# Six operations in place of seven for VectorE's share of a softmax exponential

## The chip, the cores and the metric

The kernel runs on one core of a Trainium2 chip. The metric is the device time of one execution in microseconds (us); a figure for a kernel is the median of its runs. The engines of the core are written as the profile writes them: PE (TensorE, matrix products), ACT (ScalarE, activation functions), DVE (VectorE, elementwise work), POOL (GpSimd) and SP (SyncE, which issues transfers here).

## What is computed

Two blocks are run on the same input x of 2048 tokens by 512 features, in bf16, and mixed by a gate per token:

```python
g = sigmoid((x * gate_w).sum(-1, keepdims=True))
# a: attention, 32 heads of 16 features
qkv = (x @ wqkv) split into q, k, v
p = softmax((q @ k^T) * 16 ** -0.5)        # 32 heads x 2048 x 2048
a = (p @ v) @ wo
# b: feed-forward, 1792 wide
b = (silu(x @ w_gate) * (x @ w_up)) @ w_down
out = g * a + (1 - g) * b
```

The expensive part is the exponential in the softmax: 32 x 2048 x 2048 = 134 million of them. A head has only 16 features, so the matrix products around an exponential are small beside it.

## The kernel before

**Units and blocks.** The attention is cut into 32 units: a unit is one of 4 blocks of 512 queries together with one of 8 groups of 4 heads. In a unit there are 16 key tiles of 128 keys and 4 heads, so 64 score blocks of 128 keys x 512 queries; over all units 2048 score blocks. A score block is one matrix product with a 64-row weight (`score`, L607), its exponential, and one matrix product with the values that adds into the unit's output `o_ps` in PSUM (`pv`, L719). The softmax denominators come from a column of ones in the values.

**Two ways to an exponential.** Most blocks go in pairs to ACT (`emit_pair`, L620): two scores are written into one of two PSUM buffers `s_t` (128x1024), and one ACTIVATE with Exp makes the bf16 tile `e_t` of both. The rest goes to DVE (`emit_d`, L640): the score block is written into the single PSUM buffer `d_t`, and `first` (L659) turns it into an integer in `y_t`, which holds four such blocks (128x2048, uint16, three buffers). The integer is a bf16 bit pattern with two additional fraction bits: score x 512 log2(e) / 4, plus 512 x 127. Read as it is, its nine low bits are the fraction of the power of two, and a straight line between powers of two stands in for 2^fraction. Seven operations on the whole 128x2048 tile then correct that line by a cubic in the fraction and drop the two additional bits: the fraction `z_t` is masked out (L670), three operations and one more product make the correction `u_t` (L671 to L676), it is added to `y_t` (L677), and a multiplication by 0.25 leaves the bf16 pattern (L678), which `pv` reads as bf16. `z_t` and `u_t` have one buffer each.

**Who decides on the order.** The kernel's Python writes the order of PE, ACT and DVE by hand: `ordered` (L145) chains each instruction to the one before it on its engine. A planner keeps a clock for each engine (`plan.pe`, `plan.act`, `plan.dve`) and adds a cost written in the source for every instruction emitted. The numbers at the head of each entry of `vops` (0.73 for an operation on one tensor, 1.26 for one on two, L670 to L678) are such costs. `fill_dve` (L694) gives DVE its next piece of work whenever its clock is behind PE's: first a waiting `d_t`, then an owed piece of the side work, then one of the `vops`. `to_vector` (L1085) decides whether the next score block goes to DVE: never in the first unit, only in a unit's first 50 blocks (the first 4 in the last unit), only while fewer than three `y_t` are in work and the costs left in `vops` sum to at most 6:

```python
if not un or at_ > (50 if un < UNITS - 1 else 4) or y_live[0] >= 3 or sum(v[0] for v in vops) > 6:
    return 0
return 1
```

So the costs in `vops` set, when the kernel is built, how many of the 2048 blocks go to DVE. A finished `y_t` is put on the list `late`, and its four value products are emitted once the planner's clock says that it is ready: into the open unit's `o_ps`, or, where the unit has closed, into a buffer `x_ps` of its own, which DVE adds to the unit's sum (L747).

**Side work.** The projections of q, k and v, the gate, the feed-forward block (`gu_chain`, `down_pieces`), the normalization and the output projection are cut into pieces with due times, and `Pacer` (L47) feeds them to PE in between. They take a Tanh on ACT (`th`, L557) and evacuations from PSUM on DVE (`gs`, `mt`, `bblk` and others). PE runs its instructions in order, so a product that waits for DVE holds up the scores behind it.

Of the kernel before, what the change touches and what calls it, by code (L numbers as in the profile page):

```python
# [9 lines left out]
ALU = mybir.AluOpType  # L10
# [68 lines left out]
def kernel(  # L79
# [37 lines left out]

    EXP_A = 512.0 * inv_sqrt_dh * math.log2(math.e)  # L120
    EXP_B = 512.0 * 127.0

    EXP_C3, EXP_C2, EXP_C1, EXP_S = 0.0012034477878222, 1.8215637461803453, -1248.848130748923, 1.0 / 4096.0

# [41 lines left out]
    vec = Ordered()  # L168
# [53 lines left out]
    for i in range(2):  # L222
        nc.vector.tensor_copy(
            out=wpad[i][:, :, :].rearrange("p dc (j c) -> p dc j c", c=32)[:, :, :, 1:1 + DH],
# [14 lines left out]
    for h in range(8):  # L239
# [6 lines left out]
                            op0=ALU.is_gt, op1=ALU.mult)  # L246
    nc.vector.scalar_tensor_tensor(out=bsel[:, :], in0=lo_t[:], scalar=0.5, in1=far_t[:],
                                   op0=ALU.is_lt, op1=ALU.mult)
# [34 lines left out]
    def spend(mode, mms, ready=0.0):  # L283

        plan.pe = max(plan.pe + (0.1 if mode != plan.mode else 0.0), ready) + (0.226 if mode == "F" else 0.216) * mms
        plan.mode = mode
# [320 lines left out]
    def score(ps, b):  # L607
        n, j = b // 4, HEADS[b % 4]
        (qb, g), kt = UNIT[n // KT], n % KT
        r = slice(64 * (j // 2), 64 * (j // 2) + 64)  # L610
        q = q0[qb][r, j % 2, :] if g == 0 else get_qx(qb, g // 2)[r, j % 2, g % 2, :]
        mm(ps, lhsT=kaug[r, g, kt * P:(kt + 1) * P], rhs=q, start=True, stop=True,
           tile_position=(64 * (j // 2), 0))
# [26 lines left out]
    def emit_d(b):  # L640
        while d_wait:
            pay_d()
        d_t = ps_d.tile([P, QBW], F32, tag="d", name="d_t")
        score(d_t[:, :], b)
        spend("R", 1, d_end[0])
        if not vcur:
            y_live[0] += 1
            blocks[b // (4 * KT)] = blocks.get(b // (4 * KT), 0) + 1
            vcur["y"] = vex.tile([P, NV * QBW], U16, tag="y", name="y_t", bufs=3)
            vcur["i"], vcur["b"] = 0, []  # L650
        y, i = vcur["y"], vcur["i"]
        vcur["i"] += 1
        vcur["b"].append(b)
        e_of[b] = y[:, i * QBW:(i + 1) * QBW].bitcast(BF16)
        block = dict(vcur)
        if i == NV - 1:
            vcur.clear()

        def first():  # L659
            vec.tensor_scalar(out=y[:, i * QBW:(i + 1) * QBW], in0=d_t[:, :], scalar1=EXP_A, scalar2=EXP_B,  # L660
                              op0=ALU.mult, op1=ALU.add)
            if i < NV - 1:
                return
            z = vex.tile([P, NV * QBW], U16, tag="z", name="z_t")
            u = vex.tile([P, NV * QBW], F16, tag="u", name="u_t")
            ya, za, ua = y[:, :], z[:, :], u[:, :]
            mine = list(block["b"])
            assert sorted(m % 4 for m in mine) == list(range(4)) and mine[0] // (4 * KT) == mine[-1] // (4 * KT)
            vops.extend([
                (0.73, lambda: vec.tensor_scalar(out=za, in0=ya, scalar1=0x1FF, scalar2=None, op0=ALU.bitwise_and)),  # L670
                (0.73, lambda: vec.tensor_scalar(out=ua, in0=za, scalar1=EXP_C3, scalar2=EXP_C2, op0=ALU.mult,  # L671
                                                 op1=ALU.add)),
                (1.26, lambda: vec.tensor_tensor(out=ua, in0=ua, in1=za, op=ALU.mult)),
                (0.73, lambda: vec.tensor_scalar(out=ua, in0=ua, scalar1=EXP_C1, scalar2=EXP_S, op0=ALU.add,
                                                 op1=ALU.mult)),
                (1.26, lambda: vec.tensor_tensor(out=ua, in0=ua, in1=za, op=ALU.mult)),  # L676
                (1.26, lambda: vec.tensor_tensor(out=ya, in0=ya, in1=ua, op=ALU.add)),  # L677
                (0.73, lambda: (vec.tensor_scalar(out=ya, in0=ya, scalar1=0.25, scalar2=None, op0=ALU.mult),  # L678
                                late.append((plan.dve + 0.4, mine)))),
            ])  # L680
        d_wait.append((plan.pe + 0.25, first))

    def pay_d():
        ready, f = d_wait.pop()
        plan.dve = max(plan.dve, ready) + 0.6
        f()
        d_end[0] = plan.dve + 0.1
# [189 lines left out]
    for i in range(2):  # L877
# [6 lines left out]
        if i == 0:  # L884
            vec.tensor_scalar(out=kneg1, in0=bsel0, scalar1=kpart0[:, 0:1], scalar2=None, op0=ALU.mult)
            vec.tensor_scalar(out=aq0[:, :].bitcast(U16), in0=q0r[:, :].bitcast(U16), scalar1=0x7FFF, scalar2=None,
                              op0=ALU.bitwise_and)
    vec.scalar_tensor_tensor(out=kneg0, in0=bsel0, scalar=kpart0[:, 1:2], in1=kneg1,
                             op0=ALU.mult, op1=ALU.min)
# [5 lines left out]
    for v in range(2):  # L895
        vec.scalar_tensor_tensor(out=q0[0][:, v, :], in0=bp0[:, :], scalar=vsel[:, v:v + 1],
                                 in1=q0[0][:, v, :], op0=ALU.mult, op1=ALU.add)
# [321 lines left out]
```

## Time and profile before

The kernel before takes 885.43 us (median of three runs, 884.97 to 886.7). The profiled execution has a span of 883.3 us.

| Engine | busy, us | share of the span | instructions |
|---|---|---|---|
| ACT | 853.5 | 97% | 955 |
| DVE | 797.8 | 90% | 1129 |
| PE | 784.8 | 89% | 5078 |
| POOL | 7.0 | 1% | 29 |

The first 20 us hold the loads and the first projections; then ACT starts on exponentials. After the last exponential, which starts at 873.5 us, come the last normalization, the output projection and the stores. A row of the costliest groups reads: line, engine, operation, the tile written and the tile read with shapes and types, the count; then the summed busy time and the mean of one; then the engine's idle time just before these instructions and what ended it. Instructions on one engine overlap a little, so that the mean of one can be larger than the distance from start to start. L157, L160 and L166 are the lines of the three helpers that emit every PE, ACT and DVE instruction; the tiles tell them apart.

### The profile page before, as it was taken

How to read it: one execution, taken by the hardware profiler on the slowest of the kernel's cores; microseconds unless marked ns; L12 is line 12 of the kernel's file. 1: busy time of each engine (PE TensorE's matmuls, PEld its weight loads, DVE VectorE, ACT ScalarE, POOL GpSimd, SP SyncE). 2: the span in 40 equal slices, each digit the busy share in tenths (PEclk: the TensorE clock that was granted, in tenths of full speed). 3: DMA queues.
4: the chain of work that ended last, by engine and by line, in shares of the span. 5: the costliest groups of instructions: out<-in, count | busy, mean ns of one | idle time of the engine just before them, and what ended most of it. 6: DMA issues, size and time to landing. Idle time of an engine off the chain costs nothing.

```text
span 883.3 us, 14242 instructions
## 1 busy us (share of the span) xinstructions
PE 784.8 (89%) x5078; PEld 207.2 (23%) x5168; DVE 797.8 (90%) x1129; ACT 853.5 (97%) x955; POOL 7.0 (1%) x29
## 2 busy tenths in 40 slices
PE   6999999999998898889998888998988888989876
PEld 2222222222222222222222222222222222222211
DVE  6379999999999999998999999999999999999995
ACT  3999999999999999999999999999999999999995
POOL 3000000000000000000000000000000000000000
PEclk9999999999999999999999999999999999999998
DMA  8401021121101112110001112100011111000000
GB/s 208 108 1 33 23 50 43 34 49 28 34 7 31 34 43 64 45 34 16 5 11 35 38 42 61 48 24 10 4 32 34 36 51 44 22 11 5 4 21 24
DMA packets 87535, 31.98 MB, mean 36 GB/s; under 512 B 75120, under 2 KB 87016, under 8 KB 87464
## 3 DMA queue, kind: packets, MB, share of 16 engines
q1 hardware_dynamic: 86408, 30.94, 14.3%
q8 instruction: 40, 0.66, 0.3%
q10 hardware_dynamic: 1056, 0.13, 0.1%
q14 instruction: 31, 0.25, 0.1%
HBM read 20.83 MB, written 2.34 MB: 26 GB/s over the span
## 4 chain that ended last, share of the span: by engine, by line
ACT 40%; PE 29%; DVE 17%; issue 10%; SPq 1%; DMA 1%; DVEq 0%; ACTq 0%
ACT e_t L160 37%; PE s_t L157 11%; DVE y_t L166 7%; PE o_ps L157 6%; DVE u_t L166 5%; ACT th L160 3%; PE d_t L157 3%; PE dps L157 2%; PE gp L157 2%; PE qp L157 1%; PE up L157 1%; SPq L173 1%; DVE mt L166 1%; PE kp L157 1%; DVE gs L166 1%
## 5 line engine op out<-in xcount | busy, mean ns | idle before, releaser
L160 ACT ACTIVATE e_t<-s_t 128x1024 bf16<-128x1024 f32 x890 | 830.3, 1080 | 7.0 <-PE s_t L157 6.0
L157 PE MATMUL s_t<-qx,kaug 64*128 64x512 bf16 x1668 | 333.3, 385 | 59.9 <-ACT e_t L160 55.8
L166 DVE TENSOR_SCALAR y_t<-d_t 128x512 uint16<-128x512 f32 x268 | 184.0, 687 | 28.0 <-PE d_t L157 25.1
L157 PEld LDWEIGHTS <-kaug 64*128 64x128 bf16 x2048 | 99.3, 93 | 389.3 <-issue 387.6
L157 PE MATMUL o_ps<-e_t,vaug 128*32 128x512 bf16 x1780 | 173.1, 388 | 0.9
L166 DVE TENSOR_TENSOR u_t<-u_t,z_t 128x2048 f16<-128x2048 f16 x134 | 163.4, 1219 | 1.9
L157 PE MATMUL d_t<-qx,kaug 64*128 64x512 bf16 x252 | 95.0, 377 | 1.7 <-DVE y_t L166 1.3
L166 DVE TENSOR_TENSOR y_t<-y_t,u_t 128x2048 uint16<-128x2048 uint16 x67 | 81.6, 1218 | 0.8
L157 PEld LDWEIGHTS <-vaug 128*32 128x32 bf16 x2048 | 45.4, 94 | 136.8 <-issue 133.2
L157 PE MATMUL dps<-wd_t,mt 128*128 128x512 bf16 x200 | 62.4, 384 | 3.3 <-issue 3.3
L157 PE MATMUL gp<-xT,wg 128*128 128x512 bf16 x196 | 61.6, 384 | 2.5 <-issue 2.5
L157 PE MATMUL up<-xT,wu 128*128 128x512 bf16 x210 | 62.4, 383 | 1.5 <-issue 1.4
L166 DVE TENSOR_SCALAR y_t<-y_t 128x2048 uint16<-128x2048 uint16 x67 | 46.2, 690 | 1.3
L166 DVE TENSOR_SCALAR u_t<-z_t 128x2048 f16<-128x2048 uint16 x67 | 46.0, 686 | 0.6
L166 DVE TENSOR_SCALAR u_t<-u_t 128x2048 f16<-128x2048 f16 x67 | 45.8, 684 | 0.2
L166 DVE TENSOR_SCALAR z_t<-y_t 128x2048 uint16<-128x2048 uint16 x67 | 45.9, 685 | 0.1
L166 DVE SCALAR_TENSOR_TENSOR gs<-th,gp 128x512 bf16<-128x512 bf16 x56 | 38.2, 682 | 5.1 <-ACT th L160 4.4
L166 DVE SCALAR_TENSOR_TENSOR mt<-gs,up 128x512 bf16<-128x512 bf16 x56 | 38.2, 683 | 3.5 <-PE up L157 1.7
L160 ACT ACTIVATE th<-gp 128x512 bf16<-128x512 f32 x56 | 36.8, 657 | 0.0
L157 PEld LDWEIGHTS <-mt 128*128 128x128 bf16 x263 | 16.2, 99 | 43.8 <-issue 36.8
L157 PE MATMUL s_t<-on,kaug 64*128 64x512 bf16 x112 | 22.0, 384 | 3.3 <-ACT e_t L160 3.2
L166 DVE TENSOR_TENSOR osb<-of,x_ps 128x512 bf16<-128x512 f32 x28 | 19.1, 681 | 2.8 <-PE x_ps L157 2.7
(101 smaller groups left out, 337.8 us busy)
## 6 DMA issues: line engine op xcount, KB each, us to landing
wg<-in_B_w_gate_dram SPq DMA_DIRECT2D x56, 128.0 KB
wu<-in_B_w_up_dram SPq DMA_DIRECT2D x56, 128.0 KB
on<-osb SPq DMA_DIRECT2D x120, 16.0 KB
rb<-rr SPq DMA_DIRECT2D x15, 128.0 KB
wd_t<-in_B_w_down_dram SPq DMA_DIRECT2D x1, 1792.0 KB
qx<-qst SPq DMA_DIRECT2D x112, 16.0 KB
out_dram<-o_t SPq DMA_DIRECT2D x12, 128.0 KB
kaug<-on SPq DMA_DIRECT2D x20, 64.0 KB
```

The costliest lines, as they stand in the source:

```text
L157: ordered(nc.tensor.matmul(*args, **kw))
L160: ordered(nc.scalar.activation(*args, **kw))
L166: return lambda *a, **kw: ordered(f(*a, **kw))
L173: nc.sync.dma_start_transpose(out=xT[:, dc, :], in_=x[:, dc * P:(dc + 1) * P])
```

## The change

The cubic correction is written in another form. Instead of a polynomial in the fraction z by Horner's steps, it uses w = z + 2048, made from the masked integer by an OR with 0x800 in the same instruction, and takes w times the square of a linear term of w. The square needs no further constant in between, so the operation that added C1 and scaled drops out. The constant that the new form leaves over is taken out in the last operation, where an addition joins the multiplication by 0.25, and in `EXP_B`. Seven operations on a 128x2048 tile become six; four of the six stand on the same tiles with the same shapes as before. The planner's cost list gets shorter by its 0.73. The line numbers below line 117 shift by one.

```diff
-    EXP_B = 512.0 * 127.0
-    EXP_C3, EXP_C2, EXP_C1, EXP_S = 0.0012034477878222, 1.8215637461803453, -1248.848130748923, 1.0 / 4096.0
+    EXP_K, EXP_M, EXP_D = 0.0005430666826427128, -1.2590564982977572, -43.5
+    EXP_B = 512.0 * 127.0 + (-44.13360029727899 - EXP_D)
...
-                (0.73, lambda: vec.tensor_scalar(out=za, in0=ya, scalar1=0x1FF, scalar2=None, op0=ALU.bitwise_and)),
-                (0.73, lambda: vec.tensor_scalar(out=ua, in0=za, scalar1=EXP_C3, scalar2=EXP_C2, op0=ALU.mult,
+                (0.73, lambda: vec.tensor_scalar(out=za, in0=ya, scalar1=0x1FF, scalar2=0x800, op0=ALU.bitwise_and,
+                                                 op1=ALU.bitwise_or)),
+                (0.73, lambda: vec.tensor_scalar(out=ua, in0=za, scalar1=EXP_K, scalar2=EXP_M, op0=ALU.mult,
                                                  op1=ALU.add)),
-                (1.26, lambda: vec.tensor_tensor(out=ua, in0=ua, in1=za, op=ALU.mult)),
-                (0.73, lambda: vec.tensor_scalar(out=ua, in0=ua, scalar1=EXP_C1, scalar2=EXP_S, op0=ALU.add,
-                                                 op1=ALU.mult)),
+                (1.26, lambda: vec.tensor_tensor(out=ua, in0=ua, in1=ua, op=ALU.mult)),
                 (1.26, lambda: vec.tensor_tensor(out=ua, in0=ua, in1=za, op=ALU.mult)),
                 (1.26, lambda: vec.tensor_tensor(out=ya, in0=ya, in1=ua, op=ALU.add)),
-                (0.73, lambda: (vec.tensor_scalar(out=ya, in0=ya, scalar1=0.25, scalar2=None, op0=ALU.mult),
+                (0.73, lambda: (vec.tensor_scalar(out=ya, in0=ya, scalar1=EXP_D, scalar2=0.25, op0=ALU.add,
+                                                  op1=ALU.mult),
                                 late.append((plan.dve + 0.4, mine)))),
```

## The prediction

> **What bounds the kernel now.** I first read the busy shares of the engines and their course over the span, on the profile's page.
>
> ```profile
> PE 784.8 (89%) x5078; PEld 207.2 (23%) x5168; DVE 797.8 (90%) x1129; ACT 853.5 (97%) x955; POOL 7.0 (1%) x29
> ...
> DVE  6379999999999999998999999999999999999995
> ACT  3999999999999999999999999999999999999995
> ```
>
> ACT is at nine tenths or more in every slice but the first and the last; DVE and PE are not far behind. An average does not say who waits for whom, so next the waits: engine and tile, what it waited for, total us, times, longest.
>
> ```profile
> PE s_t L157 <- ACT e_t L160: 59.0, 158, 1.0
> DVE y_t L166 <- PE d_t L157: 25.1, 55, 1.9
> ...
> ACT e_t L160 <- PE s_t L157: 6.0, 14, 1.1
> ...
> PE o_ps L157 <- DVE y_t L166: 2.4, 8, 0.6
> PE x_ps L157 <- DVE y_t L166: 2.3, 7, 0.5
> ```
>
> PE waits 59.0 us for ACT to free a score buffer; ACT waits 6.0 us for PE. DVE waits for PE, and PE waits for DVE's exponentials only 4.7 us. So the exponentials on ACT set the pace, and the time is the length of the ACT stream plus what stands before and after it. Its pace is read from ACT's timeline (start, length, instructions merged):
>
> ```profile
> 56.53 22.17 ACT L160 ACTIVATE e_t<-s_t 128x1024 bf16<-128x1024 f32 x24 [0.43 <-PE s_t L157]
> 78.60 0.59 ACT L160 ACTIVATE th<-gp 128x512 bf16<-128x512 f32 x1
> 79.07 7.45 ACT L160 ACTIVATE e_t<-s_t 128x1024 bf16<-128x1024 f32 x8
> ...
> 865.88 8.62 ACT L160 ACTIVATE e_t<-s_t 128x1024 bf16<-128x1024 f32 x9 [0.99 <-PE s_t L157]
> ```
>
> One `e_t` lasts 1.07 us (median of its tile's view), and 24 take 22.17 us, so an undisturbed one costs (22.17 - 1.07) / 23 = 0.917 us from start to start. A Tanh costs 79.07 - 78.60 = 0.47. The stream runs from 19.82 us (first `e_t`) to 865.88 + 8.62 = 874.50, which is 854.7 us. At the undisturbed pace 890 x 0.917 + 56 x 0.47 = 842.4 would do. The 12.3 us between are late starts: 6.0 show as idle time, the rest hides in the overlap of one ACTIVATE with the next. Head and tail of the span are 19.8 and 8.8 us.
>
> What a DVE exponential costs is in the groups:
>
> ```profile
> L166 DVE TENSOR_SCALAR y_t<-d_t 128x512 uint16<-128x512 f32 x268 | 184.0, 687 | 28.0 <-PE d_t L157 25.1
> ...
> L166 DVE TENSOR_TENSOR u_t<-u_t,z_t 128x2048 f16<-128x2048 f16 x134 | 163.4, 1219 | 1.9
> ...
> L166 DVE TENSOR_TENSOR y_t<-y_t,u_t 128x2048 uint16<-128x2048 uint16 x67 | 81.6, 1218 | 0.8
> ...
> L166 DVE TENSOR_SCALAR y_t<-y_t 128x2048 uint16<-128x2048 uint16 x67 | 46.2, 690 | 1.3
> L166 DVE TENSOR_SCALAR u_t<-z_t 128x2048 f16<-128x2048 uint16 x67 | 46.0, 686 | 0.6
> L166 DVE TENSOR_SCALAR u_t<-u_t 128x2048 f16<-128x2048 f16 x67 | 45.8, 684 | 0.2
> L166 DVE TENSOR_SCALAR z_t<-y_t 128x2048 uint16<-128x2048 uint16 x67 | 45.9, 685 | 0.1
> ```
>
> The reader is to see two prices: about 0.69 us for an operation on one tensor, with one arithmetic step (`y_t<-y_t`), two (`u_t<-z_t`) or a mask (`z_t`) alike, and 1.22 us for one on two tensors. The four-block tile costs 0.685 + 0.686 + 2 x 1.219 + 0.684 + 1.218 + 0.690 = 6.40 us.
>
> **What the Trainium skill says.** "VectorE: DVE Perf Modes", section "The perf-mode tier table", gives 693 ns for `tensor_scalar` and 1224 ns for `tensor_tensor` on 2048 bf16 elements; the rows above agree (684 to 690, and 1219). The section "Walkthrough: the 8-slice pipeline in each mode" says that in the 4x mode half of the slices take the first operation and the other half the second, so a second operation needs no further pass. The trace agrees for arithmetic: 686 with two steps, 690 with one. For a mask joined by an OR no row of this trace has it. "ScalarE: Activation LUTs", section "What ACT_TABLE_LOAD costs", puts an ACTIVATE with immediate operands at 186 ns + 0.833 ns an element, less 93 ns of overlap: for 1024 elements an estimate of 0.946 us. The trace shows 0.917, which I use.
>
> **The change part by part.** *The dropped operation.* At an unchanged number of DVE tiles it would take 67 x 0.684 = 45.8 us off DVE and nothing off the end: DVE waits for PE, not ACT for DVE. It counts only by what the planner does with the room.
>
> *What the planner does.* The built program's order of instructions has 71 `y_t` tiles instead of 67, so 284 score blocks go to DVE instead of 268, and 882 `e_t` instead of 890 go to ACT. Ten units now have twelve DVE blocks where six had, the rest eight as before. Tanh, side work and transfers keep their counts. The head, up to the first DVE exponentials, keeps its order.
>
> *ACT.* 8 x 0.917 = 7.3 us come off the stream that sets the end.
>
> *DVE.* The tile now costs 6.40 - 0.684 = 5.72 us if the and/or costs 0.685 as the mask did, the square 1.219 as the product did, and the last operation 0.690 with the addition. 71 x 5.72 = 406.1 against 67 x 6.40 = 428.8: -22.7. 16 more `y_t<-d_t` at 0.687: +11.0. One more addition of an `x_ps`: +0.7. Sum -11.0, so DVE goes from 797.8 to 786.8 us: about the same share of a shorter span. The unknowns: the and/or is at least 0.685; nearest rows above it are the two-tensor rate (1.22) and the `kb` reduction over 128x2048 bf16, which takes 2.28. The square with one tensor on both inputs is at least 1.218, at most that 2.28. I take the lower ends of both, since the operand types and layouts are those of the rows before.
>
> *PE.* A pair of scores costs 0.32 us (617.55 to 617.87 in the timeline), a lone `d_t` 0.30 (616.70 to 617.00). 16 x 0.30 - 8 x 0.32 = +2.2 us. Against a stream 7.3 us shorter, PE's 59.0 us of waiting for ACT shrink to about 49.5. Value products keep their number.
>
> *Late starts.* Behind a value product that waits for `y_t` the next score pair stands in PE's queue, and ACT waits for that. Where DVE is crowded this is seen: at 615.28 `x_ps` waits 0.41 us for `y_t`, at 616.10 ACT stands 0.31 us. I bound this from two sides: DVE's share is unchanged, so the 12.3 us stay; or they grow as PE's reserve shrinks, 12.3 x 59.0 / 49.5 = 14.7, so +2.4. I take +1.2.
>
> *No cost.* The new constants are immediates like the old ones. The tail after the last exponential has the same operations; the last `y_t` now stands behind the third output evacuation in DVE's order, which can hold ACT for up to about 1 us, but ACT lost 0.45 + 0.99 us there before too.
>
> Sum: 885.43 - 7.3 + 1.2 = 879.3 us.
>
> **The rivals.** *A: PE and DVE, not ACT, end the waits in the crowded stretches.* Then eight fewer `e_t` do not shorten those. For it: the chain of waits has ACT at 40% only, PE at 29%, DVE at 17%. Against it: ACT waits for PE just 6.0 us. With the gain eaten to two thirds or more, 883 to 886.5 us.
>
> *B: an operation in the new form costs more, and the time grows.* If the and/or ran at 1.22 us, DVE would get 71 x 0.535 = 38 us more, 825 in all. Between 50 and 850 us DVE has about 51 us free (800 minus the busy time of those stretches); 38 fill three quarters, and with half of it reaching PE's waits the time is 879 + 19 = 898. At 2.28 us, +113, DVE is busy for 900 us and the time is near 930; the same for the square gives +75. Against it: arithmetic pairs at 0.686.
>
> *C: fewer late starts.* A shorter chain empties DVE's queue sooner, `y_t` is ready when PE asks, and half of the 12.3 us go too: 885.4 - 7.3 - 6 = 872, or 872 to 875.5 in all. Against it: the planner fills the room with new blocks.
>
> **How the numbers follow.** Forecast (875.5 to 882.5: the bounds on the late starts, with the 1.7 us spread of the runs on either side): 0.76. A: 0.11. B: 0.06. C: 0.07. The range 875.5 to 883.0 holds the forecast and the edge of A, about 0.03 of it, so close to 0.8; what is left out lies above and below alike. Faster by over 0.2% means below 883.7: the forecast, C and 0.04 of A, together 0.87. Within 0.2%: the rest of A, 0.07. Slower: B, 0.06.
>
> **What would show it.** In the changed profile: 882 `e_t`, ACT still at 97%, `e_t` busy near 823 us; `z_t<-y_t` at 0.685 and the square at 1.219 us; DVE near 787 us; waits of ACT for PE at 5 to 9 us. If `z_t` shows 1.2 us or more, B is right. If ACT's waits for PE and its hidden late starts grow by 7 us, A is. I would be wrong altogether if the tail or the head changed by more than 2 us.

## The result and the profile after

The changed kernel takes 874.68 us (median of four runs, 874.11 to 875.78) against 885.59 for the kernel before beside it: a ratio of 0.9877, with a 95% interval of 0.986 to 0.9894. It is faster by 10.9 us. The forecast was 879.3 with a range of 875.5 to 883.0; the direction was right, the size was not, and the time lies 0.8 us below the range. One execution in the experiments below, the profiled one of e7, ran at a mean granted PE clock of 0.751 and took 957.22 us; it is left out of e7's ratio, and e7's late starts are worked out from its time instead of its profile.

The busy shares on the page of the changed kernel, with the course of DVE and ACT over the span:

```profile
PE 784.8 (90%) x5078; PEld 207.6 (24%) x5168; DVE 786.9 (90%) x1103; ACT 845.4 (97%) x947; POOL 7.1 (1%) x29
...
DVE  6379999999999999999999999999999998999984
ACT  3999999999999999999999999999999999999995
```

Nothing has changed place: ACT is at 97% as before, DVE and PE are at 90%. DVE's busy time, 786.9 us, is what the prediction worked out (786.8). The costliest groups of the changed kernel (line, engine, operation, tiles, count | busy us, mean ns | idle time before and what ended it):

```profile
L161 ACT ACTIVATE e_t<-s_t 128x1024 bf16<-128x1024 f32 x882 | 821.9, 1079 | 4.8 <-PE s_t L158 3.7
...
L167 DVE TENSOR_TENSOR u_t<-u_t 128x2048 f16<-128x2048 f16 x71 | 86.5, 1218 | 0.8
L167 DVE TENSOR_TENSOR u_t<-u_t,z_t 128x2048 f16<-128x2048 f16 x71 | 86.4, 1217 | 0.4
...
L167 DVE TENSOR_SCALAR y_t<-y_t 128x2048 uint16<-128x2048 uint16 x71 | 48.9, 688 | 1.2
...
L167 DVE TENSOR_SCALAR z_t<-y_t 128x2048 uint16<-128x2048 uint16 x71 | 48.6, 684 | 0.1
```

The reader is to see three disputed prices settled: the mask joined by an OR takes 684 ns, as the mask alone did (685); the square with one tensor on both inputs takes 1218, as the product of two tensors did (1219); the addition in the last operation costs nothing (688 against 690). The waits of the changed kernel (us in total, times, longest):

```profile
PE s_t L158 <- ACT e_t L161: 52.6, 144, 1.0
DVE y_t L167 <- PE d_t L158: 26.2, 61, 1.9
...
ACT e_t L161 <- PE s_t L158: 3.7, 8, 1.0
...
PE o_ps L158 <- DVE y_t L167: 1.7, 5, 0.5
```

ACT now waits 3.7 us for PE; it was 6.0. PE's wait for ACT went from 59.0 to 52.6 us, and still ACT starts late less, not more. ACT's timeline gives the same two landmarks as before:

```profile
19.27 36.27 ACT L161 ACTIVATE e_t<-s_t 128x1024 bf16<-128x1024 f32 x39
...
848.77 14.85 ACT L161 ACTIVATE e_t<-s_t 128x1024 bf16<-128x1024 f32 x16 [0.98 <-PE s_t L158]
```

The stream of exponentials runs from 19.27 to 848.77 + 14.85 = 863.62 us, 844.4 us long. The 16 exponentials of the second line start every (14.85 - 1.07) / 15 = 0.919 us, the pace that the prediction used (0.917). Its sum for the undisturbed pace, 882 x 0.917 + 56 x 0.47, is 835.1. So late starts are 9.2 us, where the kernel before had 12.2. With this the span's 10.9 us (883.3 to 872.4) fall into four parts (rounded):

| Part of the span | before | after | difference |
|---|---|---|---|
| head, to the first `e_t` | 19.8 | 19.3 | -0.5 |
| undisturbed stream (worked out) | 842.4 | 835.1 | -7.3 |
| late starts | 12.2 | 9.2 | -3.0 |
| tail, after the last `e_t` | 8.8 | 8.8 | 0.0 |

Eight exponentials fewer are 7.3 us, as predicted. The question for the experiments is the third row: it was forecast at +1.2 and came out at -3.0.

### The profile page after: what moved, and what is told of

The parts are those of the page before. It is cut to its first block, busy times and chain, and to the rows that moved or that the text cites. A ratio compares the mean times of both kernels' runs of the same rounds, so it can differ in the third digit from the quotient of the medians.

```text
span 872.4 us, 14196 instructions
## 1 busy us (share of the span) xinstructions
PE 784.8 (90%) x5078; PEld 207.6 (24%) x5168; DVE 786.9 (90%) x1103; ACT 845.4 (97%) x947; POOL 7.1 (1%) x29
## 3 DMA queue, kind: packets, MB, share of 16 engines
q1 hardware_dynamic: 86408, 30.94, 14.5%
## 4 chain that ended last, share of the span: by engine, by line
ACT 42%; PE 34%; DVE 11%; issue 11%; SPq 1%; DMA 0%; ACTq 0%; DVEq 0%
ACT e_t L161 38%; PE s_t L158 13%; PE o_ps L158 7%; DVE y_t L167 5%; PE d_t L158 4%; PE dps L158 3%; ACT th L161 3%; DVE u_t L167 2%; PE gp L158 2%; PE qp L158 1%; PE up L158 1%; SPq L174 1%; PE kp L158 1%; DVE mt L167 1%; PE a_ps L158 1%
## 5 line engine op out<-in xcount | busy, mean ns | idle before, releaser
L161 ACT ACTIVATE e_t<-s_t 128x1024 bf16<-128x1024 f32 x882 | 821.9, 1079 | 4.8 <-PE s_t L158 3.7
L167 DVE TENSOR_SCALAR y_t<-d_t 128x512 uint16<-128x512 f32 x284 | 195.2, 687 | 29.7 <-PE d_t L158 26.2
L158 PE MATMUL d_t<-qx,kaug 64*128 64x512 bf16 x264 | 99.6, 377 | 0.6 <-DVE y_t L167 0.3
L167 DVE TENSOR_TENSOR y_t<-y_t,u_t 128x2048 uint16<-128x2048 uint16 x71 | 86.6, 1219 | 0.9
L167 DVE TENSOR_TENSOR u_t<-u_t 128x2048 f16<-128x2048 f16 x71 | 86.5, 1218 | 0.8
L167 DVE TENSOR_TENSOR u_t<-u_t,z_t 128x2048 f16<-128x2048 f16 x71 | 86.4, 1217 | 0.4
L167 DVE TENSOR_SCALAR u_t<-z_t 128x2048 f16<-128x2048 uint16 x71 | 48.7, 687 | 0.7
L167 DVE TENSOR_SCALAR z_t<-y_t 128x2048 uint16<-128x2048 uint16 x71 | 48.6, 684 | 0.1
L158 PEld LDWEIGHTS <-wu 128*128 128x128 bf16 x224 | 13.7, 97 | 32.0 <-issue 27.6
```

What stands on the lines that cost most here:

```text
L158: ordered(nc.tensor.matmul(*args, **kw))
L161: ordered(nc.scalar.activation(*args, **kw))
L167: return lambda *a, **kw: ordered(f(*a, **kw))
```

## The experiments

Two theories stood against each other. Theory S: DVE's chain per tile is one operation shorter, so `y_t` is ready sooner, PE is held less and ACT starts late less often. Theory O, later called P: the late starts depend on how the written order falls, and the change dealt a new order. A summary of what follows. "Late, profiled" is worked out as above from first start, last end and count of `e_t` in ACT's timeline of the one profiled execution. That execution can be faster or slower than the median of its kernel, by 4.8 us in e10, so "late, median" adds the median time less the time of the profiled execution, as if all of that difference were late starts. The times of the kernel before beside these runs are 884.4 to 885.6:

| Kernel | operations | tiles | DVE busy | late, profiled | late, median | time |
|---|---|---|---|---|---|---|
| before | 7 | 67 | 797.8 | 12.2 | 12.8 | 885.6 |
| e1: old order, six operations | 6 | 67 | 757.8 | 10.9 | 10.5 | 884.67 |
| e5: old order, four operations | 4 | 67 | 610.4 | 7.1 | 9.0 | 882.12 |
| e3: before, other order | 7 | 67 | 799.1 | 18.2 | 17.4 | 890.79 |
| e7: before, third order | 7 | 66 | | | 9.8 (estimate) | 884.39 |
| changed | 6 | 71 | 786.9 | 9.2 | 9.8 | 874.68 |
| e4: changed, other order | 6 | 71 | 787.6 | 10.4 | 9.8 | 875.21 |
| e6: changed, third order | 6 | 71 | 791.4 | 13.3 | 13.3 | 878.53 |
| e9: changed, fourth order | 6 | 71 | 781.5 | 14.5 | 13.8 | 879.41 |
| e2: new order, seven operations | 7 | 71 | 825.2 | 24.8 | 25.0 | 890.10 |
| e10: before with more tiles | 7 | 70 | 817.2 | 24.5 | 19.6 | 888.65 |
| e8: changed with more tiles | 6 | 75 | 808.3 | 11.5 | 11.0 | 870.41 |
| e11: changed with more tiles | 6 | 76 | 821.3 | 28.5 | 26.3 | 884.46 |
| e12: changed with more tiles | 6 | 78 | 831.0 | 42.4 | 44.2 | 896.93 |

### e1: the new arithmetic in the old order

```diff
                 (1.26, lambda: vec.tensor_tensor(out=ua, in0=ua, in1=ua, op=ALU.mult)),
+                (0.73, lambda: None),
                 (1.26, lambda: vec.tensor_tensor(out=ua, in0=ua, in1=za, op=ALU.mult)),
```

> The six operations of the changed kernel, but the planner is still charged the 0.73 of the dropped one, so the order of PE and ACT is that of the kernel before, with 67 tiles and 890 e_t; only DVE lacks 67 x 0.684 = 45.8 us. The step as predicted (a dropped operation at an unchanged number of tiles takes nothing off the end): 885.5, within 1. Theory S (the shorter chain has y_t ready sooner, so that PE is held less and ACT starts late less often): 881.5 to 883.5, with late starts of 8 to 10 us in place of 12.2. Theory O (late starts depend on how an order happens to fall, not on the length of the chain): 885.5, within 1.

Measured: 884.67 us, a ratio of 1.0003 to the kernel before (0.9991 to 1.0016). DVE is busy for 40 us less and the time is the same. The recorded step "takes nothing off the end" stands, and theory S, which asked for 2 to 4 us less, falls for this order: the interval leaves room for a gain of 0.8 us at most. Why dropping an operation helps so little shows at the largest late start of the kernel before. Lines of its timeline, every engine (start, length):

```profile
735.05 1.22 DVE L166 TENSOR_TENSOR u_t<-u_t,z_t 128x2048 f16<-128x2048 f16 x1
...
736.19 0.68 DVE L166 TENSOR_SCALAR y_t<-d_t 128x512 uint16<-128x512 f32 x1
...
736.93 0.37 PE L157 MATMUL d_t<-qx,kaug 64*128 64x512 bf16 x1 [0.98 <-DVE y_t L166]
...
737.62 1.02 ACT L160 ACTIVATE e_t<-s_t 128x1024 bf16<-128x1024 f32 x1 [1.08 <-PE s_t L157]
```

and of e1's, at the same place in the order, where the square now stands in front:

```profile
735.13 1.22 DVE L167 TENSOR_TENSOR u_t<-u_t 128x2048 f16<-128x2048 f16 x1
...
737.01 0.37 PE L158 MATMUL d_t<-qx,kaug 64*128 64x512 bf16 x1 [0.98 <-DVE y_t L167]
...
737.70 1.02 ACT L161 ACTIVATE e_t<-s_t 128x1024 bf16<-128x1024 f32 x1 [1.08 <-PE s_t L158]
```

PE wants to write the next block into the single buffer `d_t`. DVE has yet to empty it, and the operation that empties it stands behind a product of 1.22 us. Behind PE's wait stand the next scores, and ACT starts 1.08 us late. This wait is made by what stands directly in front of one instruction, and a chain with one operation fewer elsewhere leaves it as it was. The other late starts repeat likewise: of the kernel before's eight longest, six stand in e1 within 0.01 us of their length; one is shorter (0.45 to 0.21 us) and one of 0.33 us is gone.

### e5: four operations in the old order

```diff
# against e1
-                (1.26, lambda: vec.tensor_tensor(out=ua, in0=ua, in1=ua, op=ALU.mult)),
+                (1.26, lambda: None),
                 (0.73, lambda: None),
-                (1.26, lambda: vec.tensor_tensor(out=ua, in0=ua, in1=za, op=ALU.mult)),
+                (1.26, lambda: None),
```

> As e1, and two more products are left out of the correction (the square, and its product with w), so the output is not the reference's: the chain is four operations, DVE has 67 x (0.684 + 2 x 1.219) = 209 us less than in the kernel before, and the order of PE and ACT is still that of the kernel before. Theory S (the length of DVE's chain makes the late starts): late starts fall from 12.1 to under 5 us, time 877 to 879. Theory P (late starts come from where the order puts a d_t, side work and value products in PE's queue, and from the stretch at half clock, with DVE far from full): late starts 8 to 11 us, time 882 to 885.

Measured: 882.12 us, a ratio of 0.9961 (0.9946 to 0.9975), with DVE freed of 187 us. The profile is that of the fastest of the six executions, 1.9 us below their median; its late starts are 7.1 us, at the median they would be 9.0. So some 3 us go in time, less than 2 us for each 100 us of DVE time. Theory P's range (882 to 885) just holds the time, theory S's (877 to 879) does not.

Place by place, the gain is not spread over the chain either. Of the kernel before's late starts, those of 0.58, 0.46, 0.43, 0.31 and 0.27 us stand in e5 unchanged. Gone are the largest, 1.08 us (the product of 1.22 us that stood in front is one of those left out), two of 0.35 and 0.33 us, and the two near the end, 0.45 and 0.99 us. There the kernel before runs PE at half clock in its profile, of which the last section tells more; e5's profile has no such stretch, and ACT runs through:

```profile
847.44 22.27 ACT L161 ACTIVATE e_t<-s_t 128x1024 bf16<-128x1024 f32 x24
```

### e2: seven operations in the new order

```diff
-                (1.26, lambda: vec.tensor_tensor(out=ua, in0=ua, in1=za, op=ALU.mult)),
-                (0.73, lambda: vec.tensor_scalar(out=ua, in0=ua, scalar1=EXP_C1, scalar2=EXP_S, op0=ALU.add,
-                                                 op1=ALU.mult)),
+                (1.26, lambda: (vec.tensor_tensor(out=ua, in0=ua, in1=za, op=ALU.mult),
+                                vec.tensor_scalar(out=ua, in0=ua, scalar1=EXP_C1, scalar2=EXP_S, op0=ALU.add,
+                                                  op1=ALU.mult))),
```

> The seven operations of the kernel before in the order of the changed one: 71 tiles, 882 e_t, PE and ACT in the changed kernel's order, DVE with 71 x 0.684 = 48.6 us more than there, about 835 us busy. If the room on DVE carries the gain: late starts grow well beyond 12 us, 884 or more, that is, the seven operations at 71 tiles lose what the eight fewer e_t bring. Theory S the same in kind: at least 880. Theory O: within 2 of the changed kernel, 873 to 877, since the order is the same.

Measured: 890.10 us, a ratio of 1.0062 (1.0047 to 1.0077). PE and ACT have the changed kernel's order to the last instruction, and the one operation more per tile costs about 15 us against it. Two of its waits, which read 1.7 us and 3.7 us in the changed kernel:

```profile
PE o_ps L157 <- DVE y_t L166: 9.4, 13, 1.4
...
ACT e_t L160 <- PE s_t L157: 14.4, 29, 1.1
```

So in this order the split that brings the 7.3 us can't be had without the dropped operation: with seven, DVE delivers `y_t` too late for it. Theory S had asked for this as well (at least 880): the length of the chain, which counts for little in the old order, counts in this one. Theory O, taken as "the order alone makes the late starts", falls here. What is left of it is theory P: the order makes them as long as DVE has room.

### e10: the old arithmetic with nearly the new split

The run before left one way out: the planner did not know of the seventh operation. Here it knows all of them, at lower costs.

```diff
-                (0.73, lambda: ...   # each operation on one tensor
+                (0.65, lambda: ...
-                (1.26, lambda: ...   # each operation on two tensors
+                (1.16, lambda: ...
```

> The kernel before with the planner's costs at 0.65 and 1.16 in place of 0.73 and 1.26: seven operations, 70 tiles and 884 e_t, nearly the changed kernel's split, DVE near 825 us busy. If the split alone carries the gain: 885 - 6 x 0.917 = 879.5 or below. If the sixth operation's removal is what makes room for the split, DVE at 93 to 94% holds PE and late starts take the gain back: 883 to 890.

Measured: 888.65 us, a ratio of 1.0055 (1.0038 to 1.0072), in the range put down for the second case. The late starts are 19.6 us at the median. (The 24.5 us of the profile belong to the slowest of the eleven executions, whose granted clock of 0.982 was the lowest.) Six exponentials fewer are 5.5 us, and the growth of the late starts alone is more than that. The split alone does not carry the gain.

### e3 and e7: other orders of the kernel before

```diff
# e3
-                (0.73, ... / (1.26, ...
+                (0.71, ... / (1.24, ...
# e7
-        plan.dve = max(plan.dve, ready) + 0.6
+        plan.dve = max(plan.dve, ready) + 0.58
```

> The kernel before with the planner's costs at 0.71 and 1.24 in place of 0.73 and 1.26: the arithmetic, 67 tiles and 890 e_t stay, the order falls differently (twelve-block units elsewhere, five added x_ps sums in place of three). Theory S: 885.6, within 1.5. Theory O: off by 2 to 4 us one way or the other.

> The kernel before with the planner's cost of the first operation at 0.58 in place of 0.60: seven operations, 66 tiles and 892 e_t, a third order of the old arithmetic. With the late starts of the kernel before: 884.7 + 2 x 0.917 = 886.5. Theory P: 883 to 891, in step with its late starts. If the three old orders lie at 12 us or more of late starts and the three new ones near 9, the gap is of the arithmetic and not of a lucky order.

Measured: e3 890.79 us, a ratio of 1.0069 (1.0054 to 1.0084); e7 884.39, a ratio of 0.9989 (0.9981 to 0.9998). The arithmetic is the same, e3 has the same number of tiles, and yet it takes 6 us more, more than either theory had put down. e7 has one tile less and two `e_t` more than the kernel before and is faster by 1 us; its late starts are an estimate from its time: 884.39 - 1.7 (time less span before) - 28.6 (head and tail before) - 844.3 (892 x 0.917 + 26.3) = 9.8. Most of e3's 6 us are in one place; its timeline and then its granted PE clock (the column after POOL) in two stretches:

```profile
251.73 2.28 DVE L166 TENSOR_REDUCE kb<-on 128x1 f32<-128x2048 bf16 x1
...
254.33 0.59 PE L157 MATMUL bp<-aq,kneg 128*8 128x512 bf16 x1 [2.98 <-DVE kneg L166]
...
255.56 1.94 ACT L160 ACTIVATE e_t<-s_t 128x1024 bf16<-128x1024 f32 x2 [2.96 <-PE s_t L157]
...
258.89 1.02 ACT L160 ACTIVATE e_t<-s_t 128x1024 bf16<-128x1024 f32 x1 [1.40 <-PE s_t L157]
```

```profile
249.50:253.00 3.50, 1.85 (x14) 0.34 (x12) 3.38 (x5) 3.10 (x4) 0.00 (x0) 1.00 0.34 61
253.20:259.80 6.60, 5.47 (x22) 0.98 (x22) 4.23 (x6) 2.85 (x3) 0.00 (x0) 0.50 0.06 16
```

PE waits 2.98 us for the bound `kneg`, which DVE makes from a maximum over the keys, because that reduction (2.28 us) starts only at 251.73 us, when PE already stands still. In the kernel before PE does not wait for `kneg` at all. While PE still waits, at about 253.1 us, its granted clock falls to half and stays there for 6.6 us, and ACT loses another 1.40 us and 0.37 us. The order that the costs 0.71 and 1.24 dealt leaves the exponential's arithmetic as it was; it brought the reduction and the product that needs it close together.

### e4, e6 and e9: other orders of the changed kernel

```diff
# e4
-        plan.dve = max(plan.dve, ready) + 0.6
+        plan.dve = max(plan.dve, ready) + 0.61
# e6: 7; e9: 5.5
-        if not un or ... or sum(v[0] for v in vops) > 6:
+        if not un or ... or sum(v[0] for v in vops) > 7:
```

> The changed kernel with the planner's cost of the first operation at 0.61 in place of 0.60: six operations, 71 tiles and 882 e_t stay, the order falls differently. Theory S: 874.7, within 1.5. Theory O: off by 2 to 4 us, upwards if the changed kernel's order was a lucky one.

> The changed kernel with the limit on waiting DVE work at 7 in place of 6: six operations, 71 tiles and 882 e_t stay, 13 added x_ps sums in place of four (about 6 us more on DVE), a third order. Theory S: 874.7, within 1.5. Theory P: anywhere from 872 to 880, in step with its late starts.

> The changed kernel with the limit on waiting DVE work at 5.5 in place of 6: six operations, 71 tiles, 882 e_t, three added sums, a fourth order. Theory P: the fixed parts of 71 tiles (835.1 of stream floor, 28.6 of head and tail, 2.2 from span to time) plus late starts of 8 to 14 us, as the first three new orders had 9.0, 10.3 and 13.0: 874 to 880, with the changed kernel at the low end. Theory S: 874.7, within 1.5.

Measured: 875.21 us (ratio 0.9894, 0.9879 to 0.9909), 878.53 (0.9922, 0.99 to 0.9944) and 879.41 (0.9946, 0.9924 to 0.9969). All have 71 tiles and 882 `e_t`. Theory S asked for 874.7 within 1.5 each time; e4 keeps to it, while theory O had it off by 2 to 4 us; e6 and e9 do not, and both lie in theory P's ranges. The late starts of the four orders are 9.8, 9.8, 13.3 and 13.8 us at the median. e9 has the wait for `kneg` of e3 again, 2.32 us long, followed by half clock. The changed kernel and e4 are the best of the four orders and hardly differ; the mean of the four times is 877.0.

### e8, e11 and e12: more tiles on DVE

```diff
# six operations; e8: 0.65 and 1.16, e11: 0.62 and 1.12, e12: 0.60 and 1.10
-                (0.73, ... / (1.26, ...
+                (0.65, ... / (1.16, ...
```

> The changed kernel with the planner's costs at 0.65 and 1.16, below what the operations take: 75 tiles, 874 e_t, DVE near 821 us busy. If ACT still sets the pace: 874.7 - 8 x 0.917 = 867.4. If DVE at 94 to 95% holds PE as in the run with seven operations at 71 tiles (late starts 24.8): 828 + 28.6 + 18 to 25 of late starts, 875 to 882.

> The changed kernel with the planner's costs at 0.62 and 1.12: 76 tiles, 872 e_t, 13 added sums, DVE near 820 us busy. Against the run with 75 tiles (870.4): 2 x 0.917 less if ACT sets the pace, 868.6; 870 to 874 if DVE's growing share gives it back in late starts.

> The changed kernel with the planner's costs at 0.60 and 1.10: 78 tiles, 868 e_t, DVE near 833 us busy, 96% or more. If ACT still sets the pace: 870.4 - 6 x 0.917 = 864.9. If DVE is the bound by now: late starts of 15 us or more, 869 to 880.

Measured: e8 870.41 us, a ratio of 0.9834 (0.9809 to 0.9858), so by the two ratios to the kernel before it is 0.4% faster than the changed kernel, and the best of all kernels here. It falls between what was put down for the two cases: 3 us above 867.4, of which 1.7 us are a longer tail (10.5 us after the last `e_t`). e11 takes 884.46 (0.9997, 0.9986 to 1.0009) and e12 896.93 (1.014, 1.0115 to 1.0165), both far above what was expected of them. Waits of e8:

```profile
ACT e_t L161 <- PE s_t L158: 5.3, 11, 0.7
PE o_ps L158 <- DVE y_t L167: 5.2, 10, 0.7
```

and of e12:

```profile
PE s_t L158 <- ACT e_t L161: 30.2, 74, 0.9
ACT e_t L161 <- PE s_t L158: 29.8, 49, 3.9
...
PE o_ps L158 <- DVE y_t L167: 11.6, 15, 1.5
```

In e8 ACT still sets the pace. In e12 ACT waits for PE as long as PE for ACT, PE waits for `y_t`, and each tile beyond costs far more than the two `e_t` that it saves (1.8 us). The edge is sharp: 14 us lie between 75 and 76 tiles. These two differ in more than the tile, namely in the order (13 added sums against 7) and in 13.0 us of DVE time; which of these makes the edge, these runs do not tell.

## Why the prediction missed

**What bounds the kernel: right.** ACT sets the pace before and after, at 97%. The built kernel has the eight exponentials fewer, and its undisturbed pace, 0.919, is the one that priced them at 7.3 us.

**DVE, and rival B: right.** No operation of the new form costs more than its counterpart, and DVE came to 786.9 us against 786.8. (Some luck is in that: the same operations over 71 tiles came to 781.5 to 791.4 us in the other orders.) What the Trainium skill says in "VectorE: DVE Perf Modes" on the second operation in the 4x mode holds for a mask joined by an OR too, here at 684 ns; this was the main way to a slower kernel.

**The dropped operation by itself: right.** "Nothing off the end" at an unchanged number of tiles is e1, 1.0003. The room counts only through the planner: e2 and e10 have the new split, or nearly so, without the room, and lose 5 us and 4 us to the kernel before.

**Late starts, "I take +1.2": wrong.** This is the step that failed. It bounded their change by 0 and +2.4, from DVE's unchanged share and PE's shrinking reserve, and the change was -3.0. Both bounds argued from averages. PE's reserve did shrink (59.0 to 52.6 us of waiting for ACT) with no growth of late starts, and ACT's waits for PE, expected at 5 to 9 us, fell to 3.7. The largest late starts looked at are made at single places of the written order: a `d_t` behind a long operation, a bound asked for too soon, and the stretch at half clock that comes with such a lull. A new order deals these places anew: the changed kernel has no late start of 1.08 us, and one of 0.98 us in its shorter stretch at half clock where the kernel before had 0.45 and 0.99. With 71 tiles and the same six operations the profiles show 9.2 to 14.5 us, 12.2 being the value of the kernel before, so the change of this term could have been anything from -3.0 to +2.3; the forecast 879.3 is reached by e9 (879.41), and the changed kernel, with e4, is at the lucky end.

**The range: too narrow for the same reason.** It took the spread of repeated runs, 1.7 us over three of them, for the uncertainty. Even for one order that was too little: 24 executions of the kernel before, beside e9 to e12, lie between 882.55 and 887.26. (The sum was not followed to the end either: 0 and +2.4 with 1.7 us on either side give 876.4 to 882.2, not 875.5 to 882.5.) The spread over orders is about 5 us for the new kernel (874.68 to 879.41) and about 6 for the old one (884.39 to 890.79).

**Rival C: its size nearly right, its mechanism not.** It foresaw fewer late starts and 872 to 875.5 us, and the time is in it. But it put them down to the shorter chain emptying DVE's queue sooner; e1 has the shorter chain in the old order and gains 0.8 us at most. In the new order the shorter chain is what makes the order possible (e2); whether it also has a part in the 3 us there, no run shows.

**Rival A: not seen.** ACT's waits for PE fell.

**Head and tail: right within noise.** The tail has 8.8 us in both. The 0.5 us of the head are not the change's: kernels with the same head start their first `e_t` between 19.3 and 20.8 us in these profiles, e7's aside.

What stays open: whether the new split, with DVE no fuller than before, has fewer late starts on average over orders. At the median the four orders of it have a mean of 11.7, the three of the old one 13.3 with one of them estimated, and these overlap.

## What to carry to other kernels

Where a planner written into the kernel fixes the order of the engines, an operation taken off an engine that is not the bound may pay, as here, almost only through the work that the planner then moves: count the moved instructions in the built order and price them at the bound engine's pace. Give the rest, the waits that sit at single places of the order, a range of its own from a few re-dealt orders, since costs changed by two hundredths moved the time by 6 us here (e3) without any change of arithmetic. And try a few of the planner's costs for the new operations: here 0.65 and 1.16 gave 4 us more than the costs that the change kept, while 0.62 and 1.12 gave back all of the gain.

## What had not been expected of the hardware

A short lull of PE can be paid twice. In e3 PE's granted clock fell to 0.50 at about 253.1 us, before the wait of 2.98 us had ended, and stayed there for 6.6 us (the windows above); ACT, which had lost 2.96 us by the wait, lost 1.77 us more. It takes no long gap: in the kernel before the same happens near the end, where PE had waited three times for about half a microsecond. Its windows, with the clock after POOL, before the stretch and in it:

```profile
855.00:859.60 4.60, 2.93 (x26) 0.70 (x16) 4.42 (x9) 4.60 (x7) 0.00 (x0) 1.00 0.00 2
859.80:866.40 6.60, 5.51 (x26) 1.27 (x26) 3.86 (x8) 5.16 (x6) 0.00 (x0) 0.50 0.01 2
```

PE was busy for 2.93 of 4.60 us when the clock dropped, and the 0.45 us and 0.99 us that ACT lost there, which the prediction named and left unexplained, lie in this stretch. The changed kernel has half of it, 0.50 between 846.1 and 849.4 us, with one late start of 0.98 us. "TensorE: Matmul & The Clock Gate" in the Trainium skill, section "Part 1: The HAM clock gate (the "warmup" mystery)", says that the clock is halved after an idle window of about 3.4 us and restored after a busy one. The lengths agree, about one window in the changed kernel and two in the kernel before and in e3. But the wait in e3 was shorter than a window, and in the kernel before PE was not idle at all for that long: a window that is only partly busy was enough here. How busy it has to be, these runs do not settle, but they show how close it can be. In the 3.4 us before the drop (856.3 to 859.7) PE was busy for 1.99 us; at the same place in the same order, e5 had PE busy for 2.10 us (856.7 to 860.1), and its clock stayed at 1.00. (Both records lack 90 of PE's 5168 products; e1's lacks none, and there PE was busy for 1.89 us before its drop.)

So the same order of PE's work can have such a stretch in one execution and not in the next, and the times agree with that. Of 64 executions of the kernel before beside the experiments, the 14 with a mean granted clock of 0.999 took 883.3 us in the mean, the 19 with 0.994 or less 886.1. The profiled one, with the stretch, has 0.994. That stretches like this one make the difference is likely but not shown, since no execution of this kernel at 0.999 was profiled. It also means that the late starts of a single profile can be off by 2 us or so for reasons that lie neither in the order nor in the arithmetic.
